# A fused attention and squared-ReLU kernel: the last steps of the second product between the steps of attention's last run, another first bank, another order of some sums and products, and a last block in two halves

## The chip, the cores and the metric

The kernel runs on one core of one Trainium2 chip. The metric is the device time of one execution in microseconds (us): the median over several runs. Beside it stands one execution taken by the hardware profiler; its span goes from the first to the last instruction. All durations of single instructions below come from that profiled execution.

## The reference

All inputs are float32. The batch is 8, with 12 heads, 448 positions and head size 64; the model width is 12 * 64 = 768 and the inner width is 2048.

```python
q_n, k_n = rmsnorm(q, g_q), rmsnorm(k, g_k)       # over the 64 of a head
scores = q_n @ k_n.T / sqrt(64)
attn = softmax(scores)
x = (attn @ v)                                     # to (8 * 448, 768)
h = x @ w_in                                       # 768 -> 2048, "L1"
g = maximum(h, 0) ** 2
out = g @ w_out                                    # 2048 -> 768, "L2"
```

## The kernel before

The inputs keep the scores bounded, so that of the two programs in the file the one without a row maximum runs (`attention_then_ffn_bounded`). It works in four **spans** of two batch entries each. Attention on the two entries of a span makes `xT` (the transposed x of both); the first product L1 makes `gT` (the transposed g, 128 rows by 16 column groups by 2 * 448); the second product L2 makes the output.

**L1 and L2 are done with seven block products in place of eight.** The two halves of the contraction and the two batch entries of a span make a 2 by 2 block matrix; sums of blocks are prepared (`xC`, three per half for L1, made by `combine_x`; `gC` and an overwritten quarter of `gT` for L2, made by `combine`), then seven products A11, S2, S1, S3, A12, A22, S4 follow, and their results are added up on the way out of the accumulators. In L1 (`first_product`) there are HF = 8 groups f, in each of them the seven products in the order just given, each of HC = 3 matmuls of 128 x 448 (`L1039`). They use the accumulators `pa`, `pb`, `pc`, `pd`: A11 begins `pa` and A12 adds to it; S3 begins `pd` and A22 adds to it; S1 begins `pc` and S4 adds to it. After A11 the scalar engine copies `pa` to `p1` (`L1043`), and A12 may overwrite the bank's content only after that copy; in the same way A22 may add to `pd` only after the vector engine has read S3's value (`L1054`). In L2 (`second_product`) there are 21 blocks j (`uses2`), each of HF = 8 matmuls of 128 x 448 (`L1086`) into an accumulator `ps`, and each with an addition at its end that reads it (`L1095`, `L1097`, `L1100`, `L1103`; a block S3 has two, `L1103` and `L1105`).

**Banks.** `bank(name)` hands out two accumulator banks "m" and "n" in turn, for `pb`, `pc`, `pd` and `ps`, so a block waits until the block before the last, or whoever had the bank before, has been read. In a group f of L1 the three turns are `pb`, `pc`, `pd`, and the first `ps` of L2 gets the bank that `pc` had. In span 0's attention (`attention_alone`) the `pav` of every odd head pair has bank "n".

**The order of the work is written out by hand; each engine executes its instructions in the order in which the program issues them.** `second_product` and `attention` are generators. While L2 of a span goes on, attention of the next span is issued, and after every `yield` of attention some steps of L2. A step of L2 is one matmul; blocks that also deliver an output have one step more (`deliver` transposes 128 x 448 on the vector engine, `L1074`, and issues four DMAs, `L1077`). L2 has 180 steps. Attention has 66 yields: one, and then five for each of the 12 head pairs and for a last run i = `last`, which has no new scores. The last run only sums up the 12th pair: `values` (matmuls, `L836`), a copy on the scalar engine (`L964`), `finish` (`L872` adds two accumulators, and `L874` multiplies by factors that come by DMA, `L804`), and `combine_x` (`L887` to `L889`). Before the change 160 steps of L2 are dealt out over the first 61 yields, and the last 20 are issued after attention has ended.

**Span 0's sums.** In spans 1 to 3 `combine` runs within L1. In span 0 it runs in L2: at the end of blocks 0 to 3, two groups f each with two subtractions (`L1000`, `L1001`), and at the end of blocks 4 to 7 the two others (`L1003`, `L1004`).

**Queues.** Nearly all DMAs are issued by SyncE (SP): weight blocks `sw` (`load_blocks`, five buffers, so each load waits for the matmuls of five loads ago), q, k, v, and the deliveries. The last delivery of a span alternates between SP and the scalar engine's queue.

Of the kernel before, what the change touches and what calls it, by code (L numbers as in the profile page):

```python
# [9 lines left out]
F32 = mybir.dt.float32  # L10
U32 = mybir.dt.uint32
AF = mybir.ActivationFunctionType
ALU = mybir.AluOpType
# [373 lines left out]
def attention_then_ffn_bounded(  # L387
# [35 lines left out]
    nc = tc.nc  # L423

    B, H, S, D = q.shape
    NT, DM = out.shape
    DFF = w_in.shape[1]
    P = 128
    NJ = 4
    SP = S // NJ  # L430
    NPAIR = H // 2
    NFC = DFF // P
    HALF = DM // 2
    HC = NPAIR // 2
    HF = NFC // 2
    NSPAN = B // 2
# [20 lines left out]
    turn = [0]  # L457

    def bank(name, n=None):

        turn[0] += n is None
        return ps_m.tile([P, S], F32, tag="mn"[turn[0] % 2 if n is None else n], name=name)
# [30 lines left out]
    A11, S2, S1, S3, A12, A22, S4 = range(7)  # L493
    A21 = 7
    w1s = dram.tile([HF, 7, P, HW], F32, name="w1s")
# [133 lines left out]

    uses2 = [(m, i) for m in range(HC) for i in (A11, A12)]  # L630
    uses2 += [(m, i) for m in range(HC) for i in (S2, S1, S3, A22, S4)]
    N1 = HF * 7
    N2 = HC * 7 * (HF // 4)

    def load_blocks(upto):

        while len(stream) < min(upto, NSPAN * (N1 + N2)):
            n = len(stream) % (N1 + N2)
            if written[0] < min(2 * (n // 7 + 1) if n < N1 else 2 * NFC, 2 * NFC):
                return  # L640
            sw = loads.tile([P, 4, P], F32, tag="sw", name="sw", bufs=5)
            if n < N1:
                sw = sw[:, 0:HC]
                src = w1s[n // 7, n % 7].rearrange("p (c m) -> p c m", c=HC)
            else:
                n -= N1
                m, i = uses2[n // (HF // 4)]
                src = w2s[i, n % (HF // 4), :, :, m * P:(m + 1) * P]
            nc.sync.dma_start(sw, src)
            stream.append(sw)  # L650
# [355 lines left out]
    def first_product(work, span):  # L1006

        B11, B21, B22 = xT[:, 0, 0:HC], xT[:, 0, HC:], xT[:, 1, HC:]
        T1, T2, T4, T3 = xC[:, 0], xC[:, 1], xC[:, 2], xT[:, 1, 0:HC]

        def activate(g, src):
            nc.scalar.activation(g, src, AF.Relu)  # L1012
            if span == 0:
                nc.scalar.activation(g, g, AF.Square)
            else:
                nc.gpsimd.tensor_tensor(g, g, g, ALU.mult)  # L1016

        for f in range(HF):
            n = span * (N1 + N2) + f * 7
            g11, g12 = gT[:, f, 0:S], gT[:, f, S:2 * S]  # L1020
            g21, g22 = gT[:, HF + f, 0:S], gT[:, HF + f, S:2 * S]
            add = nc.vector.tensor_tensor
            ps_of = {}
            for i in range(7):

                into, rhs = {A11: ("pa", B11), S2: ("pb", T2), S1: ("pc", T1), S3: ("pd", T3),
                             A12: ("pa", B21), A22: ("pd", T4), S4: ("pc", B22)}[i]
                first = into not in ps_of
                if first and into == "pa":
                    if span == 0 and f:  # L1030
                        ps_of[into] = ps_o.tile([P, S], F32, tag="ot"[f % 2], name="pa")
                    else:
                        ps_of[into] = ps_s.tile([P, 2, 512], F32, tag="s", name="pa")[:, 0, 0:S]
                elif first:
                    ps_of[into] = bank(into)
                ps = ps_of[into]
                load_blocks(n + i + 5)
                for c in range(HC):
                    nc.tensor.matmul(ps, stream[n + i][:, c], rhs[:, c], start=first and c == 0,  # L1039
                                     stop=c == HC - 1, skip_group_check=not first)  # L1040
                if i == A11:
                    p1 = work.tile([P, S], F32, tag="p1", name="p1", bufs=1)
                    nc.scalar.copy(p1, ps)  # L1043
                elif i == S2:
                    z = work.tile([P, S], F32, tag="z", name="z")
                    add(z, p1, ps, ALU.add)
                elif i == S1:
                    y = work.tile([P, S], F32, tag="y", name="y")
                    add(y, z, ps, ALU.add)
                elif i == A12:  # L1050
                    activate(g11, ps)
                else:
                    g, x = {S3: (g22, y), A22: (g21, z), S4: (g12, z)}[i]
                    add(g, x, ps, ALU.add)  # L1054
                    activate(g, g)
                if span and f and i in (S1, A22):
                    combine(f - 1, (int(i == A22),))
                if span and f == HF - 1 and i == S4:
                    combine(f)
                yield  # L1060

    def second_product(work, span):

        B11, B21, B22 = gT[:, 0:HF, 0:S], gT[:, HF:, 0:S], gT[:, HF:, S:2 * S]
        T1, T2, T4, T3 = gC[:, 0], gC[:, 1], gC[:, 2], gT[:, 0:HF, S:2 * S]
        rhs_of = {A11: B11, S2: T2, S1: T1, S3: T3, A12: B21, A22: T4, S4: B22}
        rows = out.rearrange("(b g t) n -> b t g n", b=B, t=32)
        n = span * (N1 + N2) + N1
        add = nc.vector.tensor_tensor
        done = []  # L1070

        def deliver(ct, col, t, queues=(nc.sync,)):
            osb = work.tile([P, S // 32, 32], F32, tag="osb", name="osb")
            nc.vector.transpose(osb.rearrange("p g n -> p (g n)"), ct)  # L1074
            for i in range(0, P, 32):
                queue = queues[i // 32 % len(queues)]
                queue.dma_start(rows[2 * span + t, :, :, col * P + i:col * P + i + 32], osb[i:i + 32])  # L1077

        p1s, c11s = {}, {}
        for j, (m, i) in enumerate(uses2):
            ps = bank("ps")
            for c in range(HF):
                load_blocks(n + 5)
                nc.tensor.matmul(ps, stream[n][:, c % 4], rhs_of[i][:, c], start=c == 0, stop=c == HF - 1)  # L1086
                n += c % 4 == 3
                if c == HF // 2 - 1 and done:
                    yield
                    deliver(*done.pop())  # L1090
                if c < HF - 1:
                    yield
            if i == A11:
                p1s[m] = work.tile([P, S], F32, tag="p1", name="p1", bufs=HC)
                nc.scalar.copy(p1s[m], ps)  # L1095
            elif i == S2:
                add(p1s[m], p1s[m], ps, ALU.add)  # L1097
            elif i == S1:
                y = work.tile([P, S], F32, tag="y", name="y", bufs=1)
                add(y, p1s[m], ps, ALU.add)  # L1100
            else:
                ct = work.tile([P, S], F32, tag="ct", name="ct", bufs=1)
                add(ct, p1s[m] if i in (A12, A22) else y, ps, ALU.add)  # L1103
                if i == S3:
                    add(p1s[m], p1s[m], ps, ALU.add)  # L1105
                done.append((ct, m + (HC if i in (S3, A22) else 0), 1 if i in (S3, S4) else 0))
            if span == 0 and j < 8:
                for f in range(j % 4 * HF // 4, (j % 4 + 1) * HF // 4):
                    combine(f, (j // 4,))
            yield  # L1110
        deliver(*done.pop(), (nc.sync, nc.scalar))
        yield


    load_v(0)
# [43 lines left out]
    for span in range(NSPAN):  # L1159
        more = span + 1 < NSPAN  # L1160
        nxt = start_of(span + 1)
        if span:
            with tc.tile_pool(name="first_product", bufs=2, reuse_waits="tile") as work:
                for u, _ in enumerate(first_product(work, span)):
                    if more:
                        ahead(u, nxt)
        with tc.tile_pool(name="second_product", bufs=2, reuse_waits="tile") as work:
            rest = second_product(work, span)
            if more:
                places_for(work, NJ)  # L1170
                places.append(qkT[:, 1])
                halves[:] = [work.tile([P, 2, S // 2], F32, tag=f"half{m}", name="half", bufs=1) for m in range(2)]
                sums_for(work)
                total, done = HC * (7 * HF + 4) - 20, 0
                for u, _ in enumerate(attention(nxt)):
                    while done < min(total, total * (u + 1) // (10 * NPAIR + 1)):
                        next(rest)
                        done += 1
            for _ in rest:
                pass  # L1180
# [89 lines left out]
```

## Time and profile before

| | |
|---|---|
| median of 3 runs | 1368.19 us (1366.46 to 1371.15) |
| the profiled execution's own time | 1369.76 us |
| its span, first to last instruction | 1367.8 us |
| granted TensorE clock, mean | 0.998 of full speed |
| TensorE (PE) busy | 1341.9 us, 98% |
| VectorE (DVE) busy | 811.9 us, 59% |
| GpSimd (POOL) busy | 633.2 us, 46% |
| ScalarE (ACT) busy | 426.8 us, 31% |
| the chain that ended last: PE's share | 86% |

A line of the timeline gives the start in us, the length in us, the engine, the line of the kernel, the operation with output and inputs, the shape, and how many instructions were merged into the line; a bracket at its end tells how long the engine had been idle before it and what the profile takes for the releaser. "PEld" is TensorE's weight load, "SPq" and "ACTq" are the queues' DMA issues. Every float32 matmul appears as two instructions: a block of L2 is 16 of them, and the start of one follows the start of the one before by 0.376 us (a line of 16 that begins at 446.31 us is 6.18 us long, and the last instruction of it is 0.545 us long). A wait for several semaphores is put down to the one that came last by the profile, so the engine named is not always the one that decided.

L1 of span 0 begins at about 132.8 us, L2 of span 0 at 263.9 us. L1 of spans 1, 2 and 3 begins at 460.8, 781.9 and about 1107 us, and the last span's L2, with no attention beside it, runs from 1234.0 to 1360.1 us.

### The profile page before, as it was taken

Reading aid. Unit: us, or ns where it says so; the run is one execution under the profiler, and the core shown is the slowest. Engines: PE = TensorE matmul, PEld = TensorE weight load, DVE = VectorE, ACT = ScalarE, POOL = GpSimd, SP = SyncE. Lnnn points to the kernel's source line nnn. Section 1 sums busy time; section 2 is a strip of 40 time slices with the busy share of each in tenths; the row PEclk is TensorE's granted clock in tenths of the full one; section 3 lists DMA queues with packets and bytes.
Section 4 is the critical chain, followed back from the end, with each engine's and each line's share of the span. In section 5 each row is a group of like instructions: output and inputs, shape, how many; then the busy total and the mean of one; then the engine's idle time right before and its main releaser. Section 6 shows DMA issues by size and latency. Waiting matters only on the chain.

```text
span 1367.8 us, 16894 instructions
## 1 busy us (share of the span) xinstructions
PE 1341.9 (98%) x5602; PEld 638.1 (47%) x5602; DVE 811.9 (59%) x1434; ACT 426.8 (31%) x657; POOL 633.2 (46%) x505
## 2 busy tenths in 40 slices
PE   8989999999999999999999999999999999999997
PEld 3333454444444455444444455444444445554553
DVE  6989776499986334467778523467788533332111
ACT  7875565433332011233332011233433101110000
POOL 6998887455563122555564122545666312220000
PEclk9999999999999999999999999999999999999999
DMA  9787998655675333446676433345765433333443
GB/s 245 194 234 198 329 390 291 184 117 118 133 141 126 97 86 87 102 113 136 130 140 121 111 93 87 100 110 106 157 124 114 99 91 89 90 90 101 106 114 66
DMA packets 434021, 190.12 MB, mean 139 GB/s; under 512 B 282885, under 2 KB 430725, under 8 KB 433925
## 3 DMA queue, kind: packets, MB, share of 16 engines
q1 hardware_dynamic: 425476, 180.10, 52.2%
q0 software_dynamic: 4736, 8.40, 2.4%
q8 instruction: 47, 0.77, 0.2%
q10 hardware_dynamic: 3712, 0.46, 0.2%
q14 instruction: 50, 0.40, 0.1%
HBM read 155.72 MB, written 33.16 MB: 138 GB/s over the span
## 4 chain that ended last, share of the span: by engine, by line
PE 86%; POOL 6%; DVE 4%; DMA 2%; issue 2%; ACT 1%; DVEq 0%; POOLq 0%; ACTq 0%
PE ps L1086 35%; PE pa L1039 10%; PE pd L1039 10%; PE pc L1039 10%; PE sc L759 7%; PE pav L836 6%; PE pb L1039 5%; POOL rstd L702 2%; POOL gC L566 1%; POOL gC L572 1%; DMA xT<-factors 1%; POOL qk L704 1%; DMA sw<-w1s 1%; ACT gT L771 0%; PE tot L850 0%
## 5 line engine op out<-in xcount | busy, mean ns | idle before, releaser
L1086 PE MATMUL ps<-gT,sw 128*128 128x448 f32 x768 | 301.1, 545 | 4.7 <-DVE p L1105 4.0
L1016 POOL TENSOR_TENSOR gT<-gT 128x448 f32<-128x448 f32 x96 | 93.9, 980 | 290.6 <-ACT gT L1012 290.6
L1086 PE MATMUL ps<-gC,sw 128*128 128x448 f32 x576 | 225.2, 542 | 0.0
L1086 PEld LDWEIGHTS ps<-gT,sw 128*128 128x128 f32 x768 | 144.4, 191 | 156.3 <-issue 145.6
L724 POOL TENSOR_TENSOR half<-half,mhalf 128x28 f32<-128x28 f32 x36 | 174.5, 4847 | 75.3 <-DVE half L723 72.1
L1086 PEld LDWEIGHTS ps<-gC,sw 128*128 128x128 f32 x576 | 108.0, 190 | 113.0 <-issue 110.1
L1039 PE MATMUL pa<-xT,sw 128*128 128x448 f32 x384 | 154.9, 539 | 0.0
L1012 ACT ACTIVATE gT<-gT 128x448 f32<-128x448 f32 x96 | 55.4, 577 | 311.6 <-DVE gT L1054 311.5
L761 ACT ACTIVATE pr<-sc 128x896 f32<-128x896 f32 x87 | 77.4, 915 | 121.5 <-PE sc L759 121.5
L759 PE MATMUL sc<-qkT 64*64 64x448 f32 (+1 forms) x1152 | 109.7, 496 | 0.0
L1039 PEld LDWEIGHTS pa<-xT,sw 128*128 128x128 f32 x384 | 72.9, 190 | 71.7 <-issue 70.3
L804 POOL DMA_DIRECT2D xT<-factors x72 | 38.0, 532 | 90.1 <-DMA factors<-square 61.0
L1054 DVE TENSOR_TENSOR gT<-z,pd 128x448 f32<-128x448 f32 x32 | 19.8, 620 | 99.7 <-PE pd L1039 99.6
L1039 PE MATMUL pb<-xC,sw 128*128 128x448 f32 x192 | 77.6, 540 | 1.4 <-issue 1.4
L1039 PE MATMUL pc<-xT,sw 128*128 128x448 f32 x192 | 77.5, 540 | 0.5 <-DMA sw<-w1s 0.5
L1039 PE MATMUL pd<-xT,sw 128*128 128x448 f32 x192 | 77.8, 541 | 0.0
L1039 PE MATMUL pc<-xC,sw 128*128 128x448 f32 x192 | 77.5, 540 | 0.0
L1039 PE MATMUL pd<-xC,sw 128*128 128x448 f32 x192 | 77.4, 539 | 0.0
L726 POOL TENSOR_TENSOR qk<-qk,half 128x448 f32<-128x448 f32 x72 | 75.0, 1061 | 2.8
L572 POOL TENSOR_TENSOR gC<-gC 128x384 f32<-128x384 f32 x64 | 73.2, 1162 | 2.5
L836 PE MATMUL pav<-pr,vt 64*64 64x448 f32 x348 | 72.7, 537 | 1.5 <-DVE half L872 1.5
L836 PE MATMUL rest<-pr,vt 64*64 64x448 f32 x348 | 72.7, 537 | 0.0
(135 smaller groups left out, 1879.7 us busy)
## 6 DMA issues: line engine op xcount, KB each, us to landing
sw<-w1s SPq DMA_DIRECT2D x224, 192.0 KB, 2.4
sw<-w2s SPq DMA_DIRECT2D x168, 256.0 KB, 3.2
w1s<-gC SPq DMA_DIRECT2D x8, 1344.0 KB, 7.5
w2s<-gC SPq DMA_DIRECT2D x8, 1344.0 KB, 8.1
out_dram<-osb SPq DMA_DIRECT2D x184, 56.0 KB, 1.9
qk<-in_q_dram SPq DMA_DIRECT2D x144, 56.0 KB, 3.6
qk<-in_k_dram SPq DMA_DIRECT2D x144, 56.0 KB, 2.9
xT<-factors POOLq DMA_DIRECT2D x72, 112.0 KB, 3.4
```

The source lines that it names most:

```text
L572: nc.gpsimd.tensor_tensor(*[blocks_of(n)[:, i] for i in (dst, x, y)], op)
L702: nc.gpsimd.tensor_tensor(flat, flat, mhalf[:SP, 0:4 * NJ], ALU.pow)
L724: nc.gpsimd.tensor_tensor(half, half, mhalf, ALU.pow)
L726: nc.gpsimd.tensor_tensor(qkn[:, s], raw[:, s], half[:, s * NG:(s + 1) * NG].rearrange("p g -> p g ()").to_broadcast([P, NG, 32]), ALU.mult)
L759: nc.tensor.matmul(sc[part, h, 0:n], qkT[rows, 0, 1, keys], qkT[rows, 0, 0, of], start=True, stop=True)
L761: nc.scalar.activation(pr, sc[:, :, 0:n], AF.Exp)
L804: nc.gpsimd.dma_start(xT[h * D:(h + 1) * D, b % 2, hp], sums["out"][i % 2].rearrange("(h g) t -> h () (g t)", h=2)[h].to_broadcast([D, S]))
L836: nc.tensor.matmul(into, vs[i][rows, h, c, :], probs[i, c][rows, h, :], start=(c == 0), stop=(c == NF), skip_group_check=True)
L1012: nc.scalar.activation(g, src, AF.Relu)
L1016: nc.gpsimd.tensor_tensor(g, g, g, ALU.mult)
L1039: nc.tensor.matmul(ps, stream[n + i][:, c], rhs[:, c], start=first and c == 0, stop=c == HC - 1, skip_group_check=not first)
L1086: nc.tensor.matmul(ps, stream[n][:, c % 4], rhs_of[i][:, c], start=c == 0, stop=c == HF - 1)
```

## The change

Five things change.

- **L2 beside attention's last run**: after the 61st yield three steps of L2 are issued after each of the five yields of the last run. Five steps remain after attention instead of 20.
- **First bank of L2**: `second_product` advances the turn once at its start, so its first `ps` has the bank that `pd` had, and all further ones are exchanged as well.
- **Span 0's sums of g**: in each of the blocks 0 to 7 one group f is combined after the second matmul and one after the sixth, not both after the block's addition.
- **First products of L1**: in span 0, group f = 0, the order is A11, A12, S2, S1, S3, A22, S4; the weight blocks are loaded in the same order.
- **Last block**: in the last span the 21st block is issued as two halves of 224 columns, each into a bank of its own and each added, transposed and delivered by itself; the delivery of block 20 goes out over two queues ahead of it. The last delivery of spans 0 to 2 uses SP's queue alone.

```diff
--- before.py
+++ after.py
@@ -629,6 +629,10 @@
 
     uses2 = [(m, i) for m in range(HC) for i in (A11, A12)]
     uses2 += [(m, i) for m in range(HC) for i in (S2, S1, S3, A22, S4)]
+    def order_of(span, f):
+
+        return (A11, A12, S2, S1, S3, A22, S4) if span == f == 0 else range(7)
+
     N1 = HF * 7
     N2 = HC * 7 * (HF // 4)
 
@@ -641,7 +645,7 @@
             sw = loads.tile([P, 4, P], F32, tag="sw", name="sw", bufs=5)
             if n < N1:
                 sw = sw[:, 0:HC]
-                src = w1s[n // 7, n % 7].rearrange("p (c m) -> p c m", c=HC)
+                src = w1s[n // 7, order_of(len(stream) // (N1 + N2), n // 7)[n % 7]].rearrange("p (c m) -> p c m", c=HC)
             else:
                 n -= N1
                 m, i = uses2[n // (HF // 4)]
@@ -1017,11 +1021,12 @@
 
         for f in range(HF):
             n = span * (N1 + N2) + f * 7
+            order = order_of(span, f)
             g11, g12 = gT[:, f, 0:S], gT[:, f, S:2 * S]
             g21, g22 = gT[:, HF + f, 0:S], gT[:, HF + f, S:2 * S]
             add = nc.vector.tensor_tensor
             ps_of = {}
-            for i in range(7):
+            for at, i in enumerate(order):
 
                 into, rhs = {A11: ("pa", B11), S2: ("pb", T2), S1: ("pc", T1), S3: ("pd", T3),
                              A12: ("pa", B21), A22: ("pd", T4), S4: ("pc", B22)}[i]
@@ -1034,9 +1039,9 @@
                 elif first:
                     ps_of[into] = bank(into)
                 ps = ps_of[into]
-                load_blocks(n + i + 5)
+                load_blocks(n + at + 5)
                 for c in range(HC):
-                    nc.tensor.matmul(ps, stream[n + i][:, c], rhs[:, c], start=first and c == 0,
+                    nc.tensor.matmul(ps, stream[n + at][:, c], rhs[:, c], start=first and c == 0,
                                      stop=c == HC - 1, skip_group_check=not first)
                 if i == A11:
                     p1 = work.tile([P, S], F32, tag="p1", name="p1", bufs=1)
@@ -1068,18 +1073,37 @@
         n = span * (N1 + N2) + N1
         add = nc.vector.tensor_tensor
         done = []
-
-        def deliver(ct, col, t, queues=(nc.sync,)):
-            osb = work.tile([P, S // 32, 32], F32, tag="osb", name="osb")
-            nc.vector.transpose(osb.rearrange("p g n -> p (g n)"), ct)
+        turn[0] += 1
+
+        def deliver(ct, col, t, queues=(nc.sync,), part=slice(0, S // 32)):
+            osb = work.tile([P, S // 32, 32], F32, tag="osb", name="osb")[:, part]
+            nc.vector.transpose(osb.rearrange("p g n -> p (g n)"), ct[:, part.start * 32:part.stop * 32])
             for i in range(0, P, 32):
                 queue = queues[i // 32 % len(queues)]
-                queue.dma_start(rows[2 * span + t, :, :, col * P + i:col * P + i + 32], osb[i:i + 32])
+                queue.dma_start(rows[2 * span + t, :, part, col * P + i:col * P + i + 32], osb[i:i + 32])
+
+        def last_block(n, m):
+
+            deliver(*done.pop(), (nc.sync, nc.scalar))
+            load_blocks(n + 5)
+            rhs = rhs_of[S4]
+            ct = work.tile([P, S], F32, tag="ct", name="ct", bufs=1)
+            half = S // 64 * 32
+            for part in (slice(0, half), slice(half, S)):
+                ps = bank("ps")[:, part]
+                for c in range(HF):
+                    nc.tensor.matmul(ps, stream[n + c // 4][:, c % 4], rhs[:, c, part],
+                                     start=c == 0, stop=c == HF - 1)
+                add(ct[:, part], y[:, part], ps, ALU.add)
+                deliver(ct, m, 1, (nc.sync, nc.scalar), slice(part.start // 32, part.stop // 32))
 
 
 
         p1s, c11s = {}, {}
         for j, (m, i) in enumerate(uses2):
+            if span == NSPAN - 1 and j == len(uses2) - 1:
+                last_block(n, m)
+                break
             ps = bank("ps")
             for c in range(HF):
                 load_blocks(n + 5)
@@ -1088,6 +1112,8 @@
                 if c == HF // 2 - 1 and done:
                     yield
                     deliver(*done.pop())
+                if span == 0 and j < 8 and c % 4 == 1:
+                    combine(j % 4 * HF // 4 + c // 4, (j // 4,))
                 if c < HF - 1:
                     yield
             if i == A11:
@@ -1104,12 +1130,10 @@
                 if i == S3:
                     add(p1s[m], p1s[m], ps, ALU.add)
                 done.append((ct, m + (HC if i in (S3, A22) else 0), 1 if i in (S3, S4) else 0))
-            if span == 0 and j < 8:
-                for f in range(j % 4 * HF // 4, (j % 4 + 1) * HF // 4):
-                    combine(f, (j // 4,))
             yield
-        deliver(*done.pop(), (nc.sync, nc.scalar))
-        yield
+        if done:
+            deliver(*done.pop())
+            yield
 
 
     load_v(0)
@@ -1171,9 +1195,9 @@
                 places.append(qkT[:, 1])
                 halves[:] = [work.tile([P, 2, S // 2], F32, tag=f"half{m}", name="half", bufs=1) for m in range(2)]
                 sums_for(work)
-                total, done = HC * (7 * HF + 4) - 20, 0
+                total, done, most = HC * (7 * HF + 4) - 20, 0, 10 * NPAIR + 1
                 for u, _ in enumerate(attention(nxt)):
-                    while done < min(total, total * (u + 1) // (10 * NPAIR + 1)):
+                    while done < total * min(u + 1, most) // most + 3 * max(u + 1 - most, 0):
                         next(rest)
                         done += 1
             for _ in rest:
```

## The prediction

> **What bounds the kernel now.** I read the page first: TensorE is busy for 1341.9 of 1367.8 us, so it sets the time, and the change can win only what TensorE idles: 25.9 us. Next, TensorE's own list of waits, to see which idle times the edits touch.
>
> ```profile
> PE 1341.9 (98%) x5602; PEld 638.1 (47%) x5602; DVE 811.9 (59%) x1434; ACT 426.8 (31%) x657; POOL 633.2 (46%) x505
> ```
> ```profile
> PE ps L1086 <- DVE p L1105: 4.0, 2, 2.0
> ...
> PE pav L836 <- DVE half L872: 1.5, 1, 1.5
> PE pb L1039 <- issue: 1.4, 1, 1.4
> ...
> PE ps L1086 <- POOL gT L1016: 0.8, 1, 0.8
> ```
>
> These four rows, 7.7 us, and the tail after the last matmul, 7.7 us, are what the five edits can reach. The rest (start, attention of span 0, one late weight block of 0.5 us) they don't touch. Then the timeline around each.
>
> End of span 0 (the same picture at 1099 us; in the middle span, at 769 us, there is no wait):
>
> ```profile
> 450.85 0.62 DVE L874 TENSOR_TENSOR xT<-half,xT 128x448 f32<-128x448 f32 x1 [4.00 <-DMA xT<-factors]
> ...
> 453.31 0.61 DVE L1103 TENSOR_TENSOR ct<-y,ps 128x448 f32<-128x448 f32 x1
> 453.85 0.61 DVE L1105 TENSOR_TENSOR p<-p,ps 128x448 f32<-128x448 f32 x1
> ```
> ```profile
> 446.31 6.18 PE L1086 MATMUL ps<-gC,sw 128*128 128x448 f32 x16
> 454.51 5.91 PE L1086 MATMUL ps<-gT,sw 128*128 128x448 f32 x15 [2.02 <-DVE p L1105]
> ```
>
> Block 18 was done at 446.3 us, yet its bank is read only at 453.3, because VectorE stood before L874 for a DMA and then did combine_x. Block 20 needs that bank and starts 2.02 us late.
>
> Span 0's L2, and the start of the last L2:
>
> ```profile
> 305.95 2.69 DVE L782 TENSOR_TENSOR acc<-acc,half 64x448 f32<-64x448 f32 x2
> 308.68 0.62 DVE L872 TENSOR_TENSOR half<-pav,half 128x448 f32<-128x448 f32 x1
> ```
> ```profile
> 309.36 0.59 PE L836 MATMUL pav<-pr,vt 64*64 64x448 f32 x1 [1.51 <-DVE half L872]
> ```
> ```profile
> 1233.29 0.62 DVE L1054 TENSOR_TENSOR gT<-z,pc 128x448 f32<-128x448 f32 x1 [0.56 <-PE pc L1039]
> ```
> ```profile
> 1234.01 8.51 PE L1086 MATMUL ps<-gT,sw 128*128 128x448 f32 x22 [0.76 <-POOL gT L1016]
> ```
>
> VectorE works without a pause from 283.3 us to beyond 345, and L872, which frees the `pav` bank, comes late in its queue. At 1234 the row names POOL, but POOL's square had ended at 1233.51; 1233.91 is when the read of `pc` ended, 0.1 us before TensorE went on. It is the bank.
>
> Start of L1:
>
> ```profile
> 135.37 0.53 ACT L1043 COPY p<-pa 128x448 f32<-128x448 f32 x1 [9.22 <-PE pa L1039]
> 135.72 0.96 DVE L874 TENSOR_TENSOR xT<-pav,gT 128x448 f32<-128x448 f32 x1
> 136.78 2.49 PE L1039 MATMUL pb<-xC,sw 128*128 128x448 f32 x6 [1.44 <-issue]
> ```
>
> A11 ends at 135.34; S2 starts at 136.78, 0.1 us after L874 released bank "n" at 136.68.
>
> **What the Trainium skill says.** "TensorE: Matmul & The Clock Gate", Back-to-back issue gap: N/2.4 + 2.5 ns per isolated matmul; LDWEIGHTS (loading the stationary operand): columns/1.2 ns, so 107 ns for 128. The trace agrees with the first: 0.3757 us for each of the two instructions of a 448-wide float32 matmul, which is 2*448/2.4 + 2.5 ns. "VectorE: DVE Perf Modes", The TRN2 errata: a float32 tensor_tensor takes (N+151)/0.96 ns, 624 ns for 448; L872 has 624. "SBUF — State Buffer", Who interferes with whom: a VectorE operation with two SBUF inputs is blocked while a GpSimd operation that reads SBUF holds the shared ports; the trace fits, L782's two parts take 2.69 us beside L726 on POOL, and 1.27 elsewhere. "DMA: Bandwidth & Descriptors", Anatomy of one DMA: about 2 us fixed, mostly the receipt; deliveries here land after 1.9 us (median).
>
> **The change part by part**, against the profiled execution's own 1369.76 us, of which 1367.8 are the span and 1.96 lie around it. That execution stands 1.57 us above the median of the runs, so I carry differences over to the median.
>
> *1. L2 beside the last run: -4.0 us.* No instruction is added, and TensorE's order stays: all of attention's matmuls come before the 62nd yield. The 161st step is the last matmul of block 18 and its two additions. They now stand ahead of L872, so they run at 446.4 to 447.6, and block 20 starts at 452.5, right behind block 19. Gain 2.02 + 1.96 = 3.98 us in spans 0 and 2, nothing in span 1. What is late next? Block 18's transpose (0.64 us) and addition move ahead of L872, which comes 2 us later; but L874 waits for its DMA until 450.85 anyway. L887 to L889 are done by 453.4, and the next S2 needs them at 458.5 + 2.25. Block 19's addition waits for them, 453.4 instead of 452.5; its bank is needed by `pb` at 460.7. SP's four delivery issues (1.9 us) move ahead too: the weight loads behind them start earlier than before. The last delivery's four issues on SP alone end 1 us later; the load behind them is used four products (9 us) on. If this cover failed, the wait would only move: 0 instead of -4.0. Bounds -4.0 and 0.
>
> *2. First bank: -0.76 us* in the last span; in the others two scores come first (TensorE has no gap there). `pd` was read 2.25 us earlier. If the wait was on POOL's square after all, 0.4 remains of the gain. Bounds -0.76 and -0.4.
>
> *3. Span 0's sums: -1.5 us.* The same 32 subtractions of 0.62 us. By counting steps (160 over 61 yields), before the VectorE pause at 278.25 to 279.62 (waiting for an exponential) there were 4 subtractions and are now 8: one pair falls into the pause of 2.86 us at 262.9, another into the 1.38 us. So between 279.6 and the L872 at 308.68 there are 8 instead of 12, some 4 * 0.6 = 2.4 us less, and L782 at 305.95 moves ahead of the L726 that began at 305.94, up to 1.4 us more. L872 was 1.51 us late: covered. Later L872s have as many or fewer subtractions ahead, and their slack is 2.35 us (k = 3), 0.8 (k = 4), 2.3 (k = 5). The weight images' last DMA out of `gC` was issued at 249.1 and takes 8.1 us, so the first sum at 263 needn't wait. Bounds -1.5 and, if sums land badly, +1.5.
>
> *4. Order of the first products: +0.6 us.* Gone: 1.44. New: A12 follows A11 in the same bank and waits for the copy L1043: 135.90 + 0.1 - 135.34 = 0.66 us. And A22 follows S3 in the same bank without A12 between: it waits for L1054, which before ended 0.66 us after S3's last matmul (143.78 to 144.44), with 0.1 us to go on 0.75 us. Two weight steps (L596 0.64, L601 0.95 to 1.67 us), behind L1054 in VectorE's queue before, are now ahead of it, as S3 comes one step later; they can put it off by up to 1.15 more. Lower bound 0.66 + 0.75 - 1.44 = 0.0, upper 0.66 + 1.9 - 1.44 = +1.1. I take a wait of 1.4 for A22, since VectorE has 1.5 us from S1's read to S3's end for 1.6 to 2.3 us of work: 0.66 + 1.4 - 1.44 = +0.6.
>
> *5. Last block in two: -1.0 us.* TensorE does 32 instructions of 224 columns: 0.19 us each (the two rounds of 224-wide `pav` matmuls start 0.19 apart), 6.05 instead of 6.01 us; weight loads show 190 ns each but two in 0.30, one per 0.11, so they hide. If they didn't (190 + some 50 ns), +1.6. Behind the last matmul: addition 0.62 to 0.39 (estimate from the formula above), transpose 0.65 to about 0.40, and the DMAs: in the last 7.7 us they move data from 1362.4 to 1364.6, about 1.6 us of full use of the 16 engines, of which half is left: -0.8. The issue (1.04 us for two) and the 3.2 us after the data stay. The first half's delivery is covered by the second half's matmuls. Sum -0.23 -0.25 -0.8 +0.05 + some 0.2 for small DMAs: -1.0. Bounds -1.4 and +0.9.
>
> **Sum**: -3.98 - 0.76 - 1.5 + 0.6 - 1.0 = -6.6 us. The profiled execution would have 1363.2 (span 1361.2), the median 1368.19 - 6.6 = **1361.6 us**. A measurement of this kernel tells 0.3%, 4.1 us, from no change.
>
> **Rivals.** *A: the edits in span 0 trade wait for wait.* The profile has VectorE full there, and part 4 puts two same-bank reads on TensorE's path. With part 4 at +1.1 and part 3 at +1.5: -3.98 - 0.76 - 1.0 + 2.6 = -3.1: 1365.1. Against it: the pauses at 262.9 and 278.3 are there to be filled.
> *B: the change doesn't do what it says at the span ends*: block 20 starts on time but the next L1 waits for weights or T2. Then -0.76 - 1.5 + 0.6 - 1.0 = -2.7: 1365.5. Against it: `sw` is five loads ahead, and span 1's end runs without a wait.
> *C: slower, by the ports that VectorE and POOL share.* The sums are two-input SBUF operations; one in the trace takes 1.25 us beside L726. If half of the 32 took 1.4 instead of 0.62, VectorE would fall 12.5 us behind in a stretch where it has no pause; less the 2.35 us of slack TensorE loses 10.1, against gains of 5.1 elsewhere: +5.0, 1373.2. It ends slower by over 0.3% from about 15 such sums on. Against it: only one of those I saw is slow now, as POOL's long L724 doesn't slow them.
> *D: more than forecast*: part 4 at 0, part 5 at -1.4, the start of later matmuls in span 0 easier: 1360.
>
> **How the numbers follow.** Forecast 0.64 (own range 1359.8 to 1363.8), A 0.15, B 0.09, C 0.06, D 0.06. Faster by over 0.3% (below 1364.1): the forecast, D, and little of A and B, 0.70. Within 0.3%: 0.24. Slower: C, 0.06. Range 1359.0 to 1366.5: it takes in A and B with 1 us for the runs' scatter.
>
> **What would show it.** Right: in TensorE's waits no L1105 row; no wait at the first `ps` of the last L2; no L872 row; no wait before `pb` at 137, but two short ones, before `pa` on L1043 and before `pd` on L1054, 1.4 to 2.6 us together; the tail from last matmul to end 6.7 instead of 7.7 us. Wrong: a new row of TensorE behind VectorE in 283 to 370 us, a wait on `sw` or `xC` at the start of a later L1, or 224-wide matmuls further than 0.2 us apart.

## The result, and the profile after

The changed kernel takes 1363.02 us (median of 6 runs, 1361.2 to 1364.84) against 1368.51 us (6 runs, 1366.46 to 1371.15): ratio 0.9955, 95% interval 0.9944 to 0.9965. That is 5.5 us between the medians and 6.2 us by the ratio (4.8 to 7.7 by its interval); 6.6 were forecast. The ratio is not that of the two medians, here and below, so the two can differ by up to 1 us. In a later run beside others the kernel stood at 1364.21 against 1368.73 (ratio 0.9963, 0.9949 to 0.9976: 5.1 us, 3.3 to 7.0). The profiled executions are further apart, 1369.76 and 1362.09 us (spans 1367.8 and 1360.0).

TensorE still bounds the time. First the page's line on the engines, then TensorE's own list of waits (who waited for whom: us in total, times, longest):

```profile
PE 1340.6 (99%) x5618; PEld 642.3 (47%) x5618; DVE 815.2 (60%) x1436; ACT 426.8 (31%) x657; POOL 636.8 (47%) x505
```
```profile
PE pd L1044 <- DVE gT L1059: 1.1, 1, 1.1
...
PE pa L1044 <- ACT p L1048: 0.6, 1, 0.6
PE pc L1044 <- DMA sw<-w1s: 0.4, 1, 0.4
```

No row is left of the four shown before; the two that were forecast for the new order have come. (Lines have moved: L1086 is now L1110, L1039 is L1044, L1054 is L1059, L872 is L876, L1103 and L1105 are L1129 and L1131.) A wait in such a list, and in a bracket, counts from the end of TensorE's last instruction; what it costs beyond that is in the part on why the prediction was right.

The end of span 0, VectorE and then TensorE:

```profile
446.68 0.62 DVE L1129 TENSOR_TENSOR ct<-y,ps 128x448 f32<-128x448 f32 x1 [2.63 <-PE ps L1110]
...
450.59 0.63 DVE L878 TENSOR_TENSOR xT<-half,xT 128x448 f32<-128x448 f32 x1 [1.70 <-DMA xT<-factors]
```
```profile
446.47 6.18 PE L1110 MATMUL ps<-gC,sw 128*128 128x448 f32 x16
452.49 6.18 PE L1110 MATMUL ps<-gT,sw 128*128 128x448 f32 x16
458.50 2.42 PE L1044 MATMUL pa<-xT,sw 128*128 128x448 f32 x6
```

Block 18's bank is read at once, L878 still waits for its DMA, and the two last blocks and the next L1 follow without a bracket.

Span 0's L2 on VectorE, and the start of the last L2 on TensorE:

```profile
304.52 1.27 DVE L786 TENSOR_TENSOR acc<-acc,half 64x448 f32<-64x448 f32 x2
305.82 0.62 DVE L876 TENSOR_TENSOR half<-pav,half 128x448 f32<-128x448 f32 x1
```
```profile
1224.96 2.42 PE L1044 MATMUL pc<-xT,sw 128*128 128x448 f32 x6
1227.22 5.05 PE L1110 MATMUL ps<-gT,sw 128*128 128x448 f32 x13
```

L786 is out from under POOL's read (2.69 us before), and L2 follows S4 with no gap.

The start of L1 in the new order, TensorE and then VectorE:

```profile
134.43 2.52 PE L1044 MATMUL pa<-xT,sw 128*128 128x448 f32 x6
137.57 2.52 PE L1044 MATMUL pa<-xT,sw 128*128 128x448 f32 x6 [0.62 <-ACT p L1048]
...
144.44 2.42 PE L1044 MATMUL pd<-xT,sw 128*128 128x448 f32 x6
148.01 2.52 PE L1044 MATMUL pd<-xC,sw 128*128 128x448 f32 x6 [1.15 <-DVE gT L1059]
```
```profile
145.19 0.55 DVE L596 TENSOR_SCALAR gC<-gC 128x768 uint32<-128x768 uint32 x1
145.77 1.65 DVE L601 SCALAR_TENSOR_TENSOR gC<-words,gC 128x768 uint32<-128x768 uint32 x1
147.35 0.61 DVE L1059 TENSOR_TENSOR gT<-y,pd 128x448 f32<-128x448 f32 x1
```

A12 waits for the copy, and A22 for L1059, which stands behind the two weight steps L596 and L601. L1 starts 1.6 us later than before. Attention is not changed there; the cause is the clock (last section).

The tail, first VectorE and SyncE's queue before the change, then TensorE and VectorE after it:

```profile
1360.57 0.62 DVE L1103 TENSOR_TENSOR ct<-y,ps 128x448 f32<-128x448 f32 x1 [4.71 <-PE ps L1086]
1361.23 0.65 DVE L1074 STREAM_TRANSPOSE osb<-ct 128x448 f32<-128x448 f32 x1
1361.90 1.04 SPq L1077 DMA_DIRECT2D out_dram<-osb  x2
```
```profile
1347.49 6.22 PE L1095 MATMUL ps<-gT,sw 128*128 128x224 f32 x32
```
```profile
1353.74 0.39 DVE L1097 TENSOR_TENSOR ct<-y,ps 128x224 f32<-128x224 f32 x1 [2.19 <-PE ps L1095]
1354.16 0.41 DVE L1080 STREAM_TRANSPOSE osb<-ct 128x224 f32<-128x224 f32 x1
```

The 32 instructions of 224 columns take 6.22 us where 16 of 448 took 6.18.

### The profile page after: what moved, and what is told of

The parts are those of the page before. It is cut to its first block, busy times and chain, and to the rows that moved or that the text cites. A ratio compares the mean times of both kernels' runs of the same rounds, so it can differ in the third digit from the quotient of the medians.

```text
span 1360.0 us, 16939 instructions
## 1 busy us (share of the span) xinstructions
PE 1340.6 (99%) x5618; PEld 642.3 (47%) x5618; DVE 815.2 (60%) x1436; ACT 426.8 (31%) x657; POOL 636.8 (47%) x505
## 4 chain that ended last, share of the span: by engine, by line
PE 89%; POOL 5%; DMA 2%; issue 2%; ACT 1%; SPq 0%; DVE 0%; ACTq 0%; POOLq 0%
PE ps L1110 37%; PE pd L1044 10%; PE pc L1044 10%; PE pa L1044 10%; PE sc L763 7%; PE pav L840 7%; PE pb L1044 5%; POOL gC L566 1%; POOL rstd L706 1%; POOL gC L572 1%; DMA sw<-w1s 1%; POOL qk L708 1%; PE sc L771 1%; ACT gT L775 1%; DMA qk<-in_k_dram 0%
## 5 line engine op out<-in xcount | busy, mean ns | idle before, releaser
L1110 PE MATMUL ps<-gT,sw 128*128 128x448 f32 x752 | 293.0, 543 | 0.0
L1110 PE MATMUL ps<-gC,sw 128*128 128x448 f32 x576 | 225.2, 543 | 0.0
L1110 PEld LDWEIGHTS ps<-gT,sw 128*128 128x128 f32 x752 | 141.2, 190 | 146.3 <-issue 142.1
L1110 PEld LDWEIGHTS ps<-gC,sw 128*128 128x128 f32 x576 | 108.2, 190 | 112.8 <-issue 110.4
L1044 PE MATMUL pa<-xT,sw 128*128 128x448 f32 x384 | 155.0, 540 | 0.6 <-ACT p L1048 0.6
L1044 PEld LDWEIGHTS pa<-xT,sw 128*128 128x128 f32 x384 | 73.0, 190 | 72.5 <-issue 69.9
L1059 DVE TENSOR_TENSOR gT<-z,pd 128x448 f32<-128x448 f32 x32 | 19.9, 621 | 100.3 <-PE pd L1044 100.3
L1044 PE MATMUL pd<-xC,sw 128*128 128x448 f32 x192 | 77.5, 540 | 1.1 <-DVE gT L1059 1.1
L1044 PE MATMUL pc<-xC,sw 128*128 128x448 f32 x192 | 77.5, 540 | 0.4 <-DMA sw<-w1s 0.4
L1044 PE MATMUL pd<-xT,sw 128*128 128x448 f32 x192 | 77.8, 542 | 0.1
L1044 PE MATMUL pc<-xT,sw 128*128 128x448 f32 x192 | 77.5, 540 | 0.0
L1044 PE MATMUL pb<-xC,sw 128*128 128x448 f32 x192 | 77.4, 539 | 0.0
```

What stands on the lines that cost most here:

```text
L1044: nc.tensor.matmul(ps, stream[n + at][:, c], rhs[:, c], start=first and c == 0, stop=c == HC - 1, skip_group_check=not first)
```

## The experiments

**Part 1 alone** (steps of L2 beside the last run):

```diff
-                total, done = HC * (7 * HF + 4) - 20, 0
+                total, done, most = HC * (7 * HF + 4) - 20, 0, 10 * NPAIR + 1
-                    while done < min(total, total * (u + 1) // (10 * NPAIR + 1)):
+                    while done < total * min(u + 1, most) // most + 3 * max(u + 1 - most, 0):
```


> The kernel before with part 1 alone: the last steps of L2 beside attention's last run. My theory (TensorE waits for a bank that VectorE reads too late): both waits on L1105 go and nothing takes their place, -4.0 us against before, and a little more where such a wait is followed by a stretch of half clock, so -4 to -5. Rival B (the wait only passes on to the next L1): 0, with a new wait before a later L1's first products.

1366.17 us against 1368.8: ratio 0.9984 (0.9977 to 0.9992), so 1.1 to 3.1 us, not 4. Both waits on L1105 are gone from its trace, and no new one has come before a later L1, so rival B falls; yet the gain is about half of the waits in the one profiled execution of before. The next runs tell why.

**Part 3 alone** (span 0's sums within the blocks):

```diff
                     deliver(*done.pop())
+                if span == 0 and j < 8 and c % 4 == 1:
+                    combine(j % 4 * HF // 4 + c // 4, (j // 4,))
...
-            if span == 0 and j < 8:
-                for f in range(j % 4 * HF // 4, (j % 4 + 1) * HF // 4):
-                    combine(f, (j // 4,))
```


> The kernel before with part 3 alone: span 0's sums after the second and sixth matmul of a block. My theory: the wait of 1.5 us on L872 goes, -1.5 us. Rival A: the wait goes elsewhere, 0 or up to +1; rival C: sums under POOL's reads, TensorE rows behind VectorE, slower by some us.

1366.96 us: ratio 0.9986 (0.9979 to 0.9994), 0.8 to 2.9 us less. The L872 row is gone; it was there with 1.5 to 1.6 us in each of the five profiles with the old sums (before, and parts 1, 2, 4 and 5 alone). Rivals A and C fall for this part.

This kernel also has the old end of spans. TensorE's waits there, first in this run, then in the one with part 4 alone (L1107 and L1110 are the L1105 of before):

```profile
PE ps L1086 <- DVE p L1107: 2.4, 2, 1.6
```
```profile
PE ps L1091 <- DVE p L1110: 1.6, 1, 1.6
```

With part 5 alone the same row has 1.9 us, with part 2 alone 1.9. The profile of before, with 4.0, was the largest of five; their mean is 2.4 us, which fits part 1's measured 1.1 to 3.1. What differs is VectorE's L874, which waits for the factors' DMA. From ScalarE's copy L964 to L874 it is 5.18 us at the end of span 0 in the profile of before (wait 2.02), 4.70 to 4.88 in the other four (waits 1.51 to 1.72); at the end of span 2 it is 5.15 (wait 1.96), 4.02 (0.84), 3.56 (0.38), 3.40 (0.21) and 3.19 (none). The wait is what this stretch has beyond some 3.17 us. So it is not a fixed price of the order but the part of a DMA chain that sticks out, and it changes from one execution to the next. What makes that chain longer or shorter stays open.

**Part 5 alone** (the last block in two halves):

```diff
...
+            if span == NSPAN - 1 and j == len(uses2) - 1:
+                last_block(n, m)
+                break
...
```


> The kernel before with part 5 alone: the last block in two halves. My theory: the tail from the end of the last matmul to the end goes from 7.3 to 6.3 us, the 32 half matmuls cost 0.05 us, together -1.0 us. Rival: weight loads don't hide behind 224 columns, the block takes 7.6 instead of 6.2 us, +0.6.

1367.89 us: ratio 0.9996 (0.9987 to 1.0006), between 1.8 us less and 0.8 more: inconclusive by time. (In this run the last delivery of spans 0 to 2 still goes out over two queues; sending it over SP's alone was run only within the whole change.) By the traces, the weight loads hide (6.2 us for the block), and from the last matmul to the end of the last transpose it is 0.87 us in place of 1.34 in every run. The rest is not shorter as a rule. From that transpose to the end the five kernels with a whole block need 5.80 to 5.89 us; the eight with two halves of 224 need 5.34, 5.44, 5.47, 6.04, 6.06, 6.13, 6.14 and 6.58. In the five longer ones the second of each queue's two DMA issues takes 1.1 to 1.5 us, where it takes 0.45 to 0.75 in the other three. One of each, SyncE's two issues in the changed kernel and in the changed kernel with the old order (5.44 and 6.58 us):

```profile
1354.60 0.81 SPq L1083 DMA_DIRECT2D out_dram<-osb  x2
```
```profile
1354.17 1.88 SPq L1083 DMA_DIRECT2D out_dram<-osb  x2
```

It does not hang on the kernel: a second profile of the changed kernel has 6.14 us. Why it is so in some executions is open. From the last matmul to the end the mean is 7.19 us with a whole block and 6.77 with two halves.

**Part 2 alone** (the turn of the banks):

```diff
         done = []
+        turn[0] += 1
```


> The kernel before with part 2 alone: the turn of the banks advanced at the start of L2. My theory (the wait at the last L2's start is for the bank that the vector engine reads, though the row names POOL): the wait of 0.76 us goes, -0.76 us, too little for a timing, so the trace decides. If the wait was for POOL's square: 0.4 us of wait stay.

1368.82 us against 1368.43, ratio 0.9996 (0.9984 to 1.0007): too small for the timing, in which even the sign differs between the medians and the ratio. Its trace has no wait at the start of the last L2, so the whole 0.76 us was the bank's, and POOL, which the row named, had nothing to do with it.

**Part 4 alone** (the order), **and the changed kernel with the old order** (the edit shown is that of the second):

```diff
-        return (A11, A12, S2, S1, S3, A22, S4) if span == f == 0 else range(7)
+        return range(7)
```


> The kernel before with part 4 alone: the other order of the first products. My theory: the wait of 1.44 us before pb goes, about 0.6 us before pa and about 1.1 us before pd come, +0.3 us. Rival: a gain of 1 us or more, as the order's purpose would have it.

> The changed kernel with the seven products of span 0's f = 0 in their old order. My theory, from the changed kernel's trace: its two short waits (0.62 + 1.15) cost 0.33 us more than the old one (1.44), so this kernel is 0.3 us faster than the changed one: -5.8 us against before. If the order as such is a gain, it is slower than the changed kernel by 1 us or more: -4.5.

Alone 1368.44 us against 1368.43 (ratio 1.0001, 0.9989 to 1.0014); the changed kernel without it 1362.72 against 1368.8 (ratio 0.9959, 0.9945 to 0.9973). Neither timing tells 0.3 us. In the traces the seven products with their waits take 17.62 us before, 17.85 to 18.02 in the five other profiles with the old order (the mean of the six is 17.90), and 18.19 or 18.20 in four profiles with the new one: 0.2 to 0.6 us longer, 0.3 in the mean. The order by itself brings nothing.

**Could another order win?** The changed kernel, with S1 between A11 and A12 and S4 between S3 and A22:

```diff
-        return (A11, A12, S2, S1, S3, A22, S4) if span == f == 0 else range(7)
+        return (A11, S1, A12, S2, S3, S4, A22) if span == f == 0 else range(7)
...
+                    turn[0] += span == f == 0 and into in ("pc", "pd")
                     ps_of[into] = bank(into)
...
```


> The changed kernel with the first seven products in the order A11, S1, A12, S2, S3, S4, A22, so that no two that share a bank stand side by side, and the turn of the banks moved so that S1 doesn't need the bank of pav. My theory: both waits (0.62 and 1.15 us) go, and none comes: 1.8 us faster than the changed kernel. Rival: VectorE is late with z and y there, and S4 or S3 waits as long as A22 did: no change.

1363.99 us (ratio 0.9971, 0.9960 to 0.9983): no gain over the changed kernel. Here S3 comes right behind S2, whose bank it takes, and waits 0.78 us for z: I had overlooked that pair. Next the order A11, S1, S2, A12, S3, S4, A22, beside the changed kernel itself:

> The changed kernel with the first seven products in the order A11, S1, S2, A12, S3, S4, A22. In the run with A12 ahead of S2, S3 came right behind S2 and waited 0.78 us for z, as both use one bank; here one product lies between every two that share a bank or wait for one another. My theory: no wait of TensorE between A11 and A22 but for a weight block, 1.8 us less waiting than the changed kernel, 1.8 us faster than it if the two are timed together. Rival: a wait comes again (VectorE, busy with combine_x until 140, is late with z), less than 1 us of gain.

> The changed kernel itself, beside the run before it and on the same chip, so that the two can be compared: 5.1 us less than before by the sum of the parts (-2.2 for the last run's steps, -1.9 for the sums, -0.8 for the bank, -0.6 to -1.0 for the last block, +0.3 for the order), between -4 and -6.5. If the parts helped each other, as the two profiled executions of before and after suggest (7.7 us apart), -7 or more.

1363.95 and 1364.21 us against 1368.73 (ratios 0.9962, 0.9948 to 0.9976, and 0.9963, 0.9949 to 0.9976): no difference. The bank waits are gone, but the sixth product now waits for its weight block. TensorE, and the queue of SyncE, in the run with this order:

```profile
146.19 2.42 PE L1045 MATMUL pd<-xT,sw 128*128 128x448 f32 x6
150.32 2.49 PE L1045 MATMUL pc<-xT,sw 128*128 128x448 f32 x6 [1.71 <-DMA sw<-w1s]
```
```profile
139.76 1.88 SPq L672 DMA_DIRECT2D qk<-in_q_dram  x4
141.74 1.99 SPq L672 DMA_DIRECT2D qk<-in_k_dram  x4
...
145.31 1.33 SPq L691 DMA_DIRECT2D vt<-in_v_dram  x2
146.73 2.08 SPq L653 DMA_DIRECT2D sw<-w1s  x4
```

The sixth block is issued 9.7 us after A11's start (137.07), behind the loads of q, k and v, and used 3.6 us later. The same 9.7 us are in the profile of before. There the sixth product started 13.06 us after A11, in the other profiles with the old order 13.26 to 13.44, in the changed kernel 13.58, with this order 13.25. Five products alone need 11.28. So behind the bank stood the queue: an order without bank waits starts the sixth product 0.3 us sooner than the changed kernel does, and at best 0.2 us sooner than the old order. A test with those loads put off by 15 products, with this order and with the old one:

```diff
-                load(NAT + 2)
...
+                if u == 14:
+                    load(NAT + 2)
+                    load_v(NAT)
```


> The order A11, S1, S2, A12, S3, S4, A22 again, and the loads of q, k and v that SyncE issues at the end of span 0's attention (load(NAT + 2), load_v(NAT)) put off by 15 products. The profiles of five kernels show the sixth weight block issued 9.7 us after A11's start, behind those loads, and landing 3.5 us later: no order can start the sixth product sooner than about 13.1 us after A11. My theory: with the loads put off the sixth block comes in time, and all waits in the first group go: some 1.8 us less waiting than the changed kernel has there, and the wait of 0.4 to 0.7 us on a weight block ten products later goes too; -7 against before where the changed kernel has -5. Rival: the block is late for another reason (the stored weights it reads, full DMA engines), and the wait stays.

> The changed kernel with the old order A11, S2, S1, S3, A12, A22, S4 and the same loads put off. My theory: the wait of 1.45 us before pb stays, as it is on pav's bank, and the sixth product starts 0.2 us or less sooner: the run with the new order is faster by 1.4 us. Rival: the wait before pb was for the queue's loads as well and goes; no difference between the two.

1367.05 and 1368.86 us against 1368.95 (ratios 0.9987, 0.9979 to 0.9995, and 0.9997, 0.9986 to 1.0007): far from the 7 us less that were expected of the first. In the first group of products the theory holds: with the loads out of the way the seven products of the new order take 15.89 us without a wait, the sixth starting after 11.38; in the old order the wait of 1.45 us before `pb` stays, and the group takes 17.57. But where the loads now stand, at 168 to 179 us, the weight stream has no more room: the run with the new order waits 4.3 us for weight blocks between 179 and 195 us, the one with the old order 3.7. As kernels both are worse than the changed one; the place for those loads wasn't found.

**Unequal halves**:

```diff
-            half = S // 64 * 32
+            half = S - 128
```


> The changed kernel with its last block divided into 320 and 128 columns instead of 224 and 224. 128 columns take 2 * 128 / 2.4 + 2.5 = 109 ns by the pace of the wider ones, and two weight loads together took 0.30 us, one per 0.11: if loads hide behind any matmul, 16 instructions take 1.75 us and the tail is 0.2 us shorter for the smaller addition and transpose, -0.2 to -0.4 us. If a load has to be waited for (190 ns each), the 16 take 3.0 us, and the kernel is 1 us slower.

1363.87 us against 1368.43, ratio 0.9963 (0.9951 to 0.9975), no difference from the changed kernel that a timing shows. Weight loads hide even behind 128 columns: the last 16 instructions start 0.112 us apart (109 ns were expected), and the whole block takes 6.25 us:

```profile
1348.71 6.25 PE L1095 MATMUL ps<-gT,sw 128*128 128x320 f32 x32
```

From the last matmul to the end it is 6.37 us where the two profiles of the changed kernel have 6.31 and 7.01. Addition and transpose take 0.2 us less; from the transpose to the end it is 5.70 us, within the 5.34 to 6.58 of equal halves, so one profile can't tell whether the smaller part gains anything.

## Why the prediction was right, and where its steps failed

The mechanism held: TensorE's waits are the account, and the four rows that the change aims at are gone. The sizes held less well, and part of the agreement is luck: steps 1 and 5 together were 2.2 us too large, and about half of that was made up by a cost of 1.0 us that no step had counted. By its steps:

| step | forecast | by the traces | by the time of that part alone |
|---|---|---|---|
| 1, last run | -4.0 | -2.4 (mean of five, 1.6 to 4.0) | -2.2 (-3.1 to -1.1) |
| 2, bank | -0.76 | -0.76 | -0.5 (-2.2 to +1.0) |
| 3, sums | -1.5 | -1.5 | -1.9 (-2.9 to -0.8) |
| 4, order | +0.6 | +0.3 (mean, 0.2 to 0.6) | +0.1 (-1.5 to +1.9) |
| 5, last block | -1.0 | -0.4 (mean): -0.5, and -0.5 to +0.7 of DMA | -0.5 (-1.8 to +0.8) |
| going on after a wait | none | -1.0 for the waits of steps 1 to 3 | in the rows above |

The times are the ratios put on 1368.4 to 1368.8 us. They add up to -5.0 us; by its own ratios the whole change has -6.2 (-7.7 to -4.8), and -5.1 (-7.0 to -3.3) in the later run. So nothing shows that the parts help or hinder each other, though with such intervals an effect of a us or two would not be seen.

**The cost that no step had.** A wait costs more than its length in the list. From the start of A11 to that of A12 in the changed kernel it is 3.14 us; six instructions at 0.376 are 2.25, and the wait is 0.62: 0.27 us are left over. In a stream an instruction of 448 columns is 0.54 us long while the next starts after 0.376, so 0.16 us of overlap is lost at a wait. The second instruction behind the wait then follows 0.45 to 0.48 us after the first, not 0.376. Both show at the waits of 2.02, 1.44 and 0.76 us before the change and at those of 0.62 and 1.15 after it: 0.24 to 0.27 us each. The change takes five waits away and brings two, and the sum of the prediction had nothing for that.

With it the two profiled executions can be accounted for: listed waits of 6.25 us gone in steps 1 to 3, an estimated 1.0 us for going on after those four, the first group 0.57 us longer, the tail 0.92 us shorter, together 7.6 of the 7.7 us between them. With the means of several profiles in place of these single draws (2.4 us for the 4.0, 0.3 for the 0.57, 0.42 for the 0.92) the same sum gives some 5.8 us, which fits the timings.

**Step 1** was mis-sized. It took "2.02 + 1.96" from one execution as if each execution paid it; in four others the second of them was 0 to 0.84. The prediction had noted that the middle span had no wait, which was the sign that this wait hangs on a DMA's arrival. What hid it afterwards is as described: the factors' DMA comes later than the two additions that moved ahead of it.

**Step 5**: "half of which is left: -0.8" failed. With half the bytes the stretch from the transpose to the end took 5.9 us in the mean of the eight profiles with equal halves, where the whole block took 5.85; what keeps it up stays open. Addition and transpose (0.39 and 0.41 us, forecast 0.39 and 0.40) are right. The step also had the end of the last matmul wrong: the tail of before is 7.2 us from 1360.5, not 7.7. The formula of the Trainium skill, "VectorE: DVE Perf Modes", The TRN2 errata, gives 391 ns for 224 columns, and L1097 has 0.39 us. That the loads hide agrees with the same skill's "TensorE: Matmul & The Clock Gate", LDWEIGHTS, whose columns/1.2 ns make 107 ns for 128 columns: 6.22 us / 32 is 0.19 us, above that. The trace lists 0.19 us for one load from start to end, but in the run with 128 columns one load follows the other after 0.112 us.

**Step 4** met its +0.6 against the one profile of before by luck: A22's wait was 1.15 us where 1.4 was taken and A12's 0.62, which makes +0.33, and the uncounted cost of one more wait makes up the rest. Against the mean of six profiles it is +0.3. Its lower bound rested on the banks alone. It priced no queue, though the loads on SyncE's queue decide what any order can win there.

**Step 3** is right to the count: 8 subtractions of 12 are left between the exponential and the L872 in question, and L782 runs in 1.27 us. **Step 2** read the right releaser behind the wrong name.

## What to carry to other kernels

When a wait ends with a DMA's arrival, its length in one profile is one draw: look at the same place in other spans and other executions before pricing it. When a wait is taken away by reordering, ask what arrives next at the same place, and go through the DMA queues for that too: here a weight block issued behind other loads came 0.2 us or less after the bank. An accumulator that is read between two adjacent groups was a wait of 0.6 to 1.2 us here, which one group of 2.25 us in between hid as long as VectorE was not busy with other work (in the new order with the loads put off it had two weight steps in front, and S3 waited 1.1 us with a group in between). And count the waits as well as adding them up: each cost some 0.25 us beyond its listed length.

## What the runs showed of the hardware

After a wait of TensorE of 1.9 to 3.2 us there sometimes came a stretch of 3.41 us at half clock; two of the 19 in the 14 profiles (those behind the last matmul not counted), at 9 us, came after one of 0.8. None came after a wait of 1.4 to 1.8 us. Here is the profile of before behind its second L1105 wait, by stretches (window, length, busy time and count of PE, PEld, DVE, ACT and POOL, granted clock, DMA share, GB/s):

```profile
1097.00:1099.00 2.00, 0.04 (x2) 0.00 (x1) 2.00 (x5) 0.00 (x0) 0.00 (x0) 1.00 0.00 0
1099.00:1100.00 1.00, 1.00 (x2) 0.63 (x3) 0.90 (x2) 0.00 (x0) 0.00 (x0) 0.71 0.00 0
1100.00:1101.00 1.00, 1.00 (x2) 0.34 (x1) 0.87 (x2) 0.00 (x0) 0.00 (x0) 0.50 0.41 70
1101.00:1102.00 1.00, 1.00 (x3) 0.56 (x2) 0.00 (x0) 0.00 (x0) 0.00 (x0) 0.50 0.63 107
1102.00:1103.00 1.00, 1.00 (x2) 0.45 (x2) 0.00 (x0) 0.00 (x0) 0.00 (x0) 0.59 0.61 90
1103.00:1104.00 1.00, 1.00 (x4) 0.57 (x3) 0.00 (x0) 0.00 (x0) 0.00 (x0) 1.00 0.99 347
```

The 16 instructions after that wait take 7.97 us in place of 6.18: a wait of 1.96 us cost some 3.8 in all. Such a stretch follows the wait at 454 us in no profile, and the one at 1099 only in this one; most of them lie in attention of span 0 (22 and 95 us), which the change doesn't touch. Between none and three were seen per execution. The start of the first L1 follows their number there: 132.8 to 132.9 us in the three profiles with none before it, 134.2 to 135.0 in the seven with one, 136.1 to 137.1 in the four with two or three. So one at 95 us is why L1 starts 1.6 us later in the profile of the changed kernel. Between the two profiled executions the stretches cancel, as each has one; what makes these two overstate the difference is the factors' wait and the tail.

The stretches do bear on the scatter of 4 to 8 us among runs of one kernel: of the 121 runs of the kernel before that were timed beside the experiments, the 18 with a mean granted clock of 0.999 took 1366.8 us in the mean, and the 15 with 0.995 took 1370.3.

The Trainium skill, "TensorE: Matmul & The Clock Gate", What's actually happening, gives an idle window of about 3.4 us before the clock falls, and about 3.4 us of sustained work before it rises. The length of the stretch at half clock agrees with the second (3.41 us). With the first it does not: a wait of 2 us was enough here, some of the time.
